# One attention-then-FFN kernel on one core: the outputs' scales in a column a chunk, k's features a slot behind q's, and some steps put first in the planner's order

## The chip, the cores and the metric

The kernel runs on one NeuronCore of a Trainium2 chip. A core has TensorE (PE, matrix products into PSUM; its weight loads are shown as PEld), VectorE (DVE), ScalarE (ACT), GpSimd (POOL) and SyncE (SP, which here issues most of the DMAs). Each engine has its own queue of instructions and takes them in order. The metric is device time of one execution in microseconds (us); lower is better.

## The reference, cut to what matters

```python
def phi(x):                                   # x: q or k, scaled by 64**-0.25
    proj = einsum('bhsd,md->bhsm', x, omega)  # 64 -> 128 features
    h = proj - sum(x * x, -1) / 2
    return exp(h - max(h, -1)) / sqrt(m)
kv  = einsum('bhsm,bhsd->bhmd', phi(k), v)
z   = sum(phi(k), over s)
num = einsum('bhsm,bhmd->bhsd', phi(q), kv)
den = einsum('bhsm,bhm->bhs',  phi(q), z) + 1e-6
x   = (num / den)  as (4608 tokens, 512)
out = ((x @ w1) * (x @ w2)) @ w3 @ w_out      # 512 -> 1024, gated, -> 512
```

8 batches, 8 heads, 576 positions, head width 64. All inputs are float32 or float64; every large product is made of float16 parts (high and low), three products for one.

## The kernel before, in words

The 4608 tokens are 36 chunks of 128. A batch is 576 tokens, that is four and a half chunks, so neighbouring batches share a chunk.

For each chunk of q and of k: a load (`load`, two buffers each of `qraw`, `kraw`), the sum of squares on ScalarE (`square_sum`, L158, tile `junk_q`/`junk_k`), its sum over partitions on TensorE and a power of two from it in four small VectorE steps (`power_of_two`, L163 to L178, and L232), the split into high and low parts (`split`, L141 on ScalarE and L144 on VectorE, tile `qhl`/`khl`), and then `features` (L250): projection on TensorE (`qpj`/`kpj`, L265), the maximum (`nm`, L275) and the subtraction (`qe`/`ke`, L288) on VectorE, the exponential on ScalarE (L289), and high and low parts again (L130, L132, L298), the low ones mostly on GpSimd.

k's features of a batch and v's parts (`vhl`) go into `kv_batch` (L339: matmuls `kvp`, L346, then high part on ScalarE, L355, and low part on VectorE, L356). q's features are transposed by DMA (`eqT`, L368) and go into `q_attend` (L370: matmuls `nu`, L381, then on VectorE gd, gr, xs, mx, L390 to L403). `x_turn` (L406) makes a power of two of mx, a scale `pt`, and the parts `xhl` (ScalarE L417, VectorE L418), which a DMA transposes into `xT` (L422).

The FFN of two chunks is four `gate` calls (48 matmuls each, L617, then asb on ScalarE and VectorE, L626 and L627, and parts on GpSimd, L631 and L632) and two `project_out` calls (24 matmuls `o`, L643). w3 and w_out are multiplied together once, in the opening (`wp`, L557), where all weights are also made from float64 words. `project_out` makes its output scale first (`osc`, L639), one number a token from `pt` and `kap`, in a small tile with four buffers; ScalarE reads it as it empties the bank (L647).

PSUM is in two pools: `ps_a`, two buffers of two banks, shared by qpj, kpj, kvp and nu; `ps_m`, four banks, shared by ab, o, the norms and the weights' products.

What sets the order. The program is written out slot by slot. Chunk step i begins at slot `begin[i]` = 3, 6, 9, ... for i = -5, -4, ... (the k chunk is i + 5, so k runs five chunks ahead of q). `put(slot, rank, fn)` files a piece of work; a slot issues its share of the weights, one unit of the FFN (`unit`), its pieces by rank, and one piece of v's work (`v_unit`). For step i: norms at begin - 3, scales at begin - 2, splits and next loads at begin - 1, q's features at begin (rank 1), k's at begin (rank 2), q_attend at begin + 5 (+ 2 for the first six), x_turn a slot after it, kv_batch five slots after its last k chunk (four or two for the first ones). v's eleven pieces of a batch (five sums, one scale, five splits) are queued when the second k chunk of the batch comes by; kv() runs what is left of them before it calls kv_batch.

That is the order of the program, and not yet that of an engine's queue. A planner plays the program through with a cost model before it is compiled; whenever an engine is free in that play, it takes the instruction that is ready there and has the lowest number, and the numbers go up in program order. The queues are then fixed. An instruction that was ready in the play and isn't on the chip makes its engine wait, with all that stands behind it. Inside `tc.high_priority()` an instruction gets the number of the program's start, so that it is taken first from the moment at which it is ready in the play.

Of the kernel before, what the change touches and what calls it, by code (L numbers as in the profile page):

```python
# [9 lines left out]
F32 = mybir.dt.float32  # L10
# [9 lines left out]
P = 128  # L20
# [30 lines left out]
EAGER = 40  # L51
EARLY = 6
KV_LAG = 5
RAW64_BUFS = 3
O_BUFS = 2
RAW_BUFS = 2
# [10 lines left out]
def tile_favor_attention_then_bilinear_ffn(  # L67
# [48 lines left out]
    def small(name, n=1, rows=P, dt=F32, bufs=4):  # L116
        return sm.tile([rows, n], dt, tag=f"s_{name}", name=name, bufs=bufs)
# [42 lines left out]
    def power_of_two(cols, n, name, pre=1.0, add=False, bufs=4):  # L160

        bank = bank_m(f"norm_{name}")
        nc.tensor.matmul(bank[:, 0:n], ones, cols, start=True, stop=True)  # L163
        t = bank[:, 0:n]
        if add:
            total = small("total")
            nc.vector.tensor_reduce(total, t, AX.X, ALU.add)
            t, n = total, 1

        q = bank[:, 16 : 16 + n]  # L170
        p = bank[:, 32 : 32 + n]

        nc.vector.tensor_scalar(
            q.bitcast(I32), t.bitcast(I32), 24, 23, ALU.logical_shift_right, ALU.logical_shift_left
        )
        nc.vector.tensor_scalar(p, q, 2.0**50 / pre, 2.0**-77 / pre, ALU.mult, ALU.max)
        s = small(f"s{n}_{bufs}", n, bufs=bufs)
        nc.vector.reciprocal(s, p)  # L178
        return p, s

    def pow2(val, n, name, bufs=4):

        p = small(f"p2p{n}_{bufs}", n, dt=I32, bufs=bufs)
        nc.vector.tensor_scalar(p, val.bitcast(I32), EXP_MASK, None, ALU.bitwise_and)
        p = p.bitcast(F32)
        r = small(f"p2r{n}_{bufs}", n, bufs=bufs)
        nc.vector.reciprocal(r, p)
        return p, r
# [150 lines left out]
    def kv_batch(b):  # L339
        t = at.tile([P, 2, H, E], F16, tag="kv", name=f"kv_{b}", bufs=3)  # L340
        cs = chunks_of(b)
        ps = banks(f"kvp_{b}")[:, :, 0 : 4 * E].rearrange("p g (i e) -> p g i e", e=E)
        for h in range(H):
            mm = [(c, x, y) for c, _, _ in cs for x, y in PASSES]
            for n, (c, x, y) in enumerate(mm):
                nc.tensor.matmul(  # L346
                    ps[:, h // 4, h % 4],
                    ek[c][:, x, place(h)],
                    vhl[b, c][:, y, h],
                    start=n == 0,  # L350
                    stop=n == len(mm) - 1,
                )
        ps = ps.rearrange("p g i e -> p g (i e)")
        hi, lo = (t[:, x].rearrange("p (g i) e -> p g (i e)", g=2) for x in range(2))
        nc.scalar.mul(hi, ps, 2.0**-19)  # L355
        nc.vector.scalar_tensor_tensor(lo, ps, 2.0**-19, hi, ALU.mult, ALU.subtract)  # L356
        kvs[b] = t

    xT, pts, eqs, xss = {}, {}, {}, {}
# [10 lines left out]
    def q_attend(c):  # L370

        t = eqs.pop(c)
        owners = [
            (b, max(b * S - c * P, 0), min((b + 1) * S - c * P, P))
            for b in range(c * P // S, ((c + 1) * P - 1) // S + 1)
        ]
        nu = banks(f"nu_{c}")[:, :, 0 : 4 * E].rearrange("p g (i e) -> p g i e", e=E)
        for h in range(H):
            for n, (x, y) in enumerate(PASSES):
                for b, r0, r1 in owners:  # L380
                    nc.tensor.matmul(  # L381
                        nu[r0:r1, h // 4, h % 4],
                        t[:, x, place(h), r0:r1],
                        kvs[b][:, y, h],
                        start=n == 0,
                        stop=n == 2,
                    )

        gd = small("gd", H)
        nc.vector.tensor_scalar_add(  # L390
            gd.rearrange("p (g i) -> p g i", g=2), nu[:, :, :, D], 1e-6 * M * 2.0**21
        )
        gr = small("gr", H)
        nc.vector.reciprocal(gr, gd)
        xs = at.tile([P, HD], F32, tag="xs", name=f"xs_{c}", bufs=1)
        nc.vector.tensor_tensor(  # L396
            xs.rearrange("p (g i d) -> p g i d", g=2, d=D),
            nu[:, :, :, 0:D],
            gr.rearrange("p (g i) -> p g i", g=2).unsqueeze(3).broadcast_to([P, 2, 4, D]),
            ALU.mult,  # L400
        )
        mx = small("mx")
        nc.vector.tensor_reduce(mx, xs, AX.X, ALU.max, apply_absolute_value=True)  # L403
        xss[c] = xs, mx, owners

    def x_turn(c):  # L406

        xs, mx, owners = xss.pop(c)
        nc.vector.tensor_scalar(mx, mx, TINY, 2.0**-12, ALU.max, ALU.mult)  # L409
        p, r = pow2(mx, 1, f"x{c}")  # L410

        pt = sm.tile([P, 1], F32, tag="pt", name=f"pt_{c}", bufs=14)
        for b, r0, r1 in owners:
            nc.vector.tensor_scalar(pt[r0:r1], p[r0:r1], pv[b][r0:r1], None, ALU.mult)
        pts[c] = pt
        t = at.tile([P, 2, HD], F16, tag="xhl", name=f"xhl_{c}", bufs=1)
        nc.scalar.mul(t[:, 0], xs, r)  # L417
        nc.vector.scalar_tensor_tensor(t[:, 1], xs, r, t[:, 0], ALU.mult, ALU.subtract)  # L418
        mc, off = c * P // TOK, c * P % TOK
        if mc not in xT:  # L420
            xT[mc] = at.tile([P, 2, NC, TOK], F16, tag="xT", name=f"xT_{mc}", bufs=XT_BUFS)
        nc.sync.dma_start_transpose(  # L422
            xT[mc].rearrange("p x c s -> p (x c) s")[:, :, off : off + P],
            t.rearrange("p x d -> p (x d)"),
        )

    w12b = const.tile([P, 2, 2 * NC + 1, 512], F32, name="w12b")
    Wb = const.tile([P, NF + 1, DO], F32, name="Wb")
# [175 lines left out]
    def gate(c0, n, u):  # L604
# [28 lines left out]
        for k in range(nf):  # L633
            for t in range(n):
                hs[c0 + t, u * nf + k] = h[:, :, k, t * P : (t + 1) * P], place

    def project_out(c):
        sc = small("osc")
        nc.vector.tensor_scalar(sc, pts[c], pts[c], kap, ALU.mult, ALU.mult)  # L639
        ps = bank_m(f"o_{c}")  # L640
        mm = [(f, a, b) for f in range(NF) for a, b in PASSES]
        for i, (f, a, b) in enumerate(mm):
            nc.tensor.matmul(ps, hs[c, f][0][:, a], W[f][:, b], start=i == 0, stop=i == len(mm) - 1)  # L643
        for f in range(NF):
            used(hs[c, f][1])
        o = mo.tile([P, DO], F32, tag="o", name=f"o_{c}", bufs=O_BUFS)
        nc.scalar.mul(o, ps, sc)  # L647
        nc.sync.dma_start(out[c * P : (c + 1) * P, :], o)
# [15 lines left out]
    def v_unit():  # L664
        if v_work:
            v_work.pop(0)[1]()
# [52 lines left out]
        plan.setdefault(slot, []).append((rank, len(plan[slot]) if slot in plan else 0, fn))  # L719

    behind_by = []

    def ready(c):
        x_turn(c)
# [14 lines left out]
    def step(i):  # L739
        at0 = begin[i]  # L740
        kc = i + LEAD
        keys = [(n, c) for n, c in (("q", i), ("k", kc)) if 0 <= c < NCH]
        state = {}

        def norms():
            state["am"] = norm(keys, i)

        def splits():
            for name, c in keys:
                split_raw(c, name)  # L750
                if c + 2 < NCH:
                    load(srcs[name], c + 2, name)

        put(at0 - 3, 3, norms)
        put(at0 - 2, 6, lambda: scale(keys, state["am"]))
        put(at0 - 1, 8, splits)
        if i >= 0:
            put(at0, 1, lambda: q_chunk(i))
            lag = 2 if i < EARLY else 5
            put(at0 + lag, 7 if i < EARLY else 0, lambda: q_attend(i))  # L760
            put(at0 + lag + 1, 0, lambda: ready(i))
        if kc < NCH:
            put(at0, 2, lambda: k_chunk(kc))
        if kc in B_OF_K:

            def kv():

                while v_work and v_work[0][0] <= B_OF_K[kc]:
                    v_unit()
                kv_batch(B_OF_K[kc])  # L770


            put(at0 + (2 if i < 0 else KV_LAG - 1 if i < EARLY else KV_LAG), 5, kv)
        for b in range(B):
            cs = [c for c, _, _ in chunks_of(b)]
            if cs[1] == kc:
                put(at0, 9, lambda b=b: v_batch(b))
            if cs[0] == kc:
                put(at0 + 2, 10, lambda cs=cs: [v_load(c) for c in cs if c not in vraw])
# [7 lines left out]
    for t in range(max(plan) + 1):  # L787
        n = min(PER[t] if t < len(PER) else 1, len(ticks))
        weights(n)
        if not ticks and raw_at:  # L790
            for a, w in [(a, 4) for a in raw_at] + [(a, 2) for a in mag_at]:
                free.extend(range(a, a + w))
            raw_at.clear()
        unit(RESERVE if t > EAGER else 0)
        for _, _, fn in sorted(plan.get(t, []), key=lambda x: x[:2]):
            fn()
        v_unit()
    assert not ticks
    while queue:
        unit()  # L800
# [38 lines left out]
```

## Time and profile before

| | |
|---|---|
| median of 3 runs | 906.85 us (904.66 to 910.05) |
| profiled execution | 904.25 us, of which the span is 902.5 us |
| mean granted TensorE clock | 0.951 |
| busy: PE / DVE / ACT / POOL | 790.9 / 622.6 / 421.0 / 322.2 us |
| DMA | 88.43 MB in 142525 packets |

All times in the profile are from the start of the span, in us. Instructions are named by engine, line of the kernel and operation, with output and input tiles by the names above; "idle before, <- X" is the time for which the engine stood still ahead of an instruction and what it waited for. Busy time of TensorE is modelled from the starts of pipelined matmuls. A clock of 1.00 is full speed.

### The profile page before, as it was taken

To read this page: it belongs to the slowest core of one execution; us is meant where nothing else is said; L and a number is where in the kernel's file an instruction comes from. 1 tells how busy PE (TensorE), PEld (TensorE's weight loads), DVE (VectorE), ACT (ScalarE), POOL (GpSimd) and SP (SyncE) were. 2 spreads that over 40 slices of the span, in tenths; PEclk is the share of its full clock that TensorE was granted. 3 is DMA by queue.
4 is the path that set the end of the run, shared out by engine and by line. 5 is a ranking of instruction groups with operands and counts; after the bars stand their busy time and mean duration, and the time that the engine had idled before them with its cause. 6 is when DMAs were issued, how large, how long until landed. Compare 5 with 4: busy or idle time off the path is not lost.

```text
span 902.5 us, 20601 instructions
## 1 busy us (share of the span) xinstructions
PE 790.9 (88%) x8614; PEld 586.0 (65%) x8614; DVE 622.6 (69%) x1116; ACT 421.0 (47%) x748; POOL 322.2 (36%) x327
## 2 busy tenths in 40 slices
PE   1964499578996998999999999899899899999998
PEld 0433254476875876767777776777677677677674
DVE  5879877788779887766867777778667774553210
ACT  3677874877436535444354335543454333221111
POOL 0000003223364465443634643455444543323221
PEclk9985699789999999999999999999999999999999
DMA  8535455332345353333434443344332232333000
GB/s 311 191 120 196 140 153 170 111 73 55 88 107 105 84 130 83 83 84 83 116 83 77 95 111 71 72 94 113 85 93 65 60 71 61 82 60 60 24 25 35
DMA packets 142525, 88.43 MB, mean 98 GB/s; under 512 B 116704, under 2 KB 116832, under 8 KB 142432
## 3 DMA queue, kind: packets, MB, share of 16 engines
q1 hardware_dynamic: 134944, 66.15, 31.0%
q10 hardware_dynamic: 7488, 20.97, 6.9%
q8 instruction: 67, 1.10, 0.5%
q14 instruction: 26, 0.21, 0.1%
HBM read 49.35 MB, written 9.44 MB: 65 GB/s over the span
## 4 chain that ended last, share of the span: by engine, by line
PE 42%; DVE 28%; ACT 13%; DMA 9%; issue 6%; POOL 1%; SPq 0%; DVEq 0%; ACTq 0%; POOLq 0%
PE ab L617 20%; PE o L643 11%; DVE nm L275 5%; DVE qhl L144 4%; DMA qraw<-qT 4%; PE wp L557 4%; DVE vhl L144 3%; ACT ke L289 2%; DVE qe L288 2%; DVE ke L288 2%; DMA kraw<-kT 2%; ACT ek L132 2%; PE kvp L346 2%; DVE asb L627 2%; PE nu L381 1%
## 5 line engine op out<-in xcount | busy, mean ns | idle before, releaser
L617 PE MATMUL ab<-xT,w12b 128*128 128x256 f16 (+1 forms) x3840 | 400.3, 265 | 10.8 <-DMA xT<-xhl 8.5
L617 PEld LDWEIGHTS <-w12b 128*128 128x128 f16 x3840 | 345.1, 99 | 54.3 <-issue 8.8
L643 PE MATMUL o<-Wb,arena 128*128 128x512 f16 x864 | 193.4, 379 | 2.1 <-DVE Wb L144 1.6
L643 PEld LDWEIGHTS <-arena 128*128 128x128 f16 x864 | 84.3, 100 | 96.3 <-issue 2.9
L631 POOL TENSOR_SCALAR arena<-asb 128x512 f16<-128x512 f32 x72 | 57.6, 800 | 249.7 <-DVE asb L627 238.3
L298 POOL TENSOR_TENSOR eq<-qe,eq 128x1024 f16<-128x1024 f32 x34 | 73.9, 2174 | 147.9 <-DVE eq L130 111.1
L289 ACT ACTIVATE qe<-qe,ln_e,es 128x1024 f32<-128x1024 f32 x31 | 38.4, 1239 | 138.0 <-DVE qe L288 138.0
L632 POOL TENSOR_TENSOR arena<-asb,arena 128x512 f16<-128x512 f32 x72 | 91.4, 1270 | 5.9
L627 DVE TENSOR_TENSOR asb<-ab,asb 128x512 f32<-128x512 f32 x72 | 49.4, 686 | 52.7 <-PE ab L617 50.6
L144 DVE SCALAR_TENSOR_TENSOR qhl<-qraw,s,qhl 128x512 f16<-128x512 f32 x36 | 63.8, 1773 | 28.7 <-ACT qhl L141 28.7
L158 ACT ACTIVATE junk_q<-qraw 128x512 bf16<-128x512 f32 x36 | 22.7, 630 | 120.4 <-DMA qraw<-qT 120.3
L298 POOL TENSOR_TENSOR ek<-ke,ek 128x1024 f16<-128x1024 f32 x28 | 60.2, 2149 | 41.4 <-DVE ek L130 39.8
L265 PE MATMUL kpj<-om,khl 64*128 64x128 f16 x864 | 36.9, 237 | 43.4 <-DVE xs L396 12.1
L639 DVE TENSOR_SCALAR osc<-pt,kap 128x1 f32<-128x1 f32 x36 | 9.5, 271 | 84.8 <-ACT o L647 84.6
L265 PEld LDWEIGHTS <-khl 64*128 64x128 f16 x864 | 29.4, 103 | 50.2 <-ACT junk_k L158 16.1
L557 PE MATMUL wp<-w12b 128*128 128x512 f32 x128 | 60.2, 623 | 1.2 <-DVE w12b L485 1.2
L626 ACT ACTIVATE asb<-ab 128x512 f32<-128x512 f32 x72 | 41.8, 580 | 24.4 <-PE ab L617 24.4
L381 PEld LDWEIGHTS <-eqT 128*128 128x128 f16 (+1 forms) x960 | 32.5, 102 | 26.0 <-DMA eqT<-eq 15.3
L647 ACT ACTIVATE o<-o,osc 128x512 f32<-128x512 f32 x36 | 24.2, 673 | 52.2 <-PE o L643 52.2
L381 PE MATMUL nu<-kv,eqT 128*128 128x65 f16 (+1 forms) x960 | 34.7, 196 | 15.0 <-DMA eqT<-eq 14.3
L418 DVE SCALAR_TENSOR_TENSOR xhl<-xs,p2r,xhl 128x512 f16<-128x512 f32 x36 | 28.8, 800 | 26.5 <-ACT xhl L417 26.4
L143 POOL TENSOR_SCALAR vhl<-vraw,s 128x512 f16<-128x512 f32 (+1 forms) x35 | 36.3, 1054 | 29.4 <-DVE mx L409 11.7
(124 smaller groups left out, 1071.1 us busy)
## 6 DMA issues: line engine op xcount, KB each, us to landing
kraw<-kT SPq DMA_DIRECT2D x36, 256.0 KB, 3.0
vraw<-v SPq DMA_DIRECT2D x36, 256.0 KB, 3.0
qraw<-qT SPq DMA_DIRECT2D x36, 256.0 KB, 2.7
out<-o SPq DMA_DIRECT2D x36, 256.0 KB, 2.0
arena<-w3T ACTq DMA_DIRECT2D x8, 1024.0 KB, 5.9
arena<-w ACTq DMA_DIRECT2D x8, 1024.0 KB, 5.6
arena<-wo ACTq DMA_DIRECT2D x4, 1024.0 KB, 5.1
eqT<-eq SPq DMA_TRANSPOSE x72, 3.1
```

The lines of the kernel that those rows point to most:

```text
L144: nc.vector.scalar_tensor_tensor(lo, src, s, hi, ALU.mult, ALU.subtract)
L265: nc.tensor.matmul(pg[:, g, i], hl[d, x, i], om[d, y], start=first is None and n == 0, stop=n == len(PASSES) - 1,)
L275: nc.vector.tensor_reduce(nm, pj, AX.X, ALU.max, negate=True)
L289: nc.scalar.activation(e, e, AF.Exp, scale=es, bias=ln_e)
L298: (nc.vector if lo == "d" else nc.gpsimd).tensor_tensor(t[:, 1], e, t[:, 0], ALU.subtract)
L381: nc.tensor.matmul(nu[r0:r1, h // 4, h % 4], t[:, x, place(h), r0:r1], kvs[b][:, y, h], start=n == 0, stop=n == 2,)
L557: nc.tensor.matmul(ps, w[:, j, k * P : (k + 1) * P], guest[:, j], start=j == j0, stop=j == HALF - 1,)
L617: nc.tensor.matmul(ps[:, k], w12[m][i][cc][:, a, r * P : (r + 1) * P], x[:, b, cc, off : off + T], start=j == 0, stop=j == len(mm) - 1,)
L627: nc.vector.tensor_tensor(asb, ab[1], asb, ALU.mult)
L631: nc.gpsimd.tensor_scalar(h[:, 0], asb, 1.0, 1.0, ALU.mult, ALU.mult)
L632: nc.gpsimd.tensor_tensor(h[:, 1], asb, h[:, 0], ALU.subtract)
L643: nc.tensor.matmul(ps, hs[c, f][0][:, a], W[f][:, b], start=i == 0, stop=i == len(mm) - 1)
```

## The change

```diff
+K_LATE = 8
...
 def power_of_two(...):
...
+        with tc.high_priority():
             q = bank[:, 16 : 16 + n]
             p = bank[:, 32 : 32 + n]
...
             nc.vector.tensor_scalar(p, q, 2.0**50 / pre, 2.0**-77 / pre, ALU.mult, ALU.max)
             s = small(f"s{n}_{bufs}", n, bufs=bufs)
             nc.vector.reciprocal(s, p)
...
 def kv_batch(b):
...
-        nc.scalar.mul(hi, ps, 2.0**-19)
-        nc.vector.scalar_tensor_tensor(lo, ps, 2.0**-19, hi, ALU.mult, ALU.subtract)
+        with tc.high_priority():
+            nc.scalar.mul(hi, ps, 2.0**-19)
+            nc.vector.scalar_tensor_tensor(lo, ps, 2.0**-19, hi, ALU.mult, ALU.subtract)
...
 def q_attend(c):
...
+        with tc.high_priority():
             gd = small("gd", H)
...
             nc.vector.tensor_reduce(mx, xs, AX.X, ALU.max, apply_absolute_value=True)
...
 def x_turn(c):
         xs, mx, owners = xss.pop(c)
+        with tc.high_priority():
             nc.vector.tensor_scalar(mx, mx, TINY, 2.0**-12, ALU.max, ALU.mult)
...
             nc.sync.dma_start_transpose(
                 xT[mc].rearrange("p x c s -> p (x c) s")[:, :, off : off + P],
                 t.rearrange("p x d -> p (x d)"),
             )
...
+    oscs = const.tile([P, NCH], F32, name="oscs")
+
     def project_out(c):
-        sc = small("osc")
+        sc = oscs[:, c : c + 1]
         nc.vector.tensor_scalar(sc, pts[c], pts[c], kap, ALU.mult, ALU.mult)
...
+    due = {}
...
-            put(at0, 2, lambda: k_chunk(kc))
+            put(at0 + (i >= K_LATE), 2, lambda: k_chunk(kc))
...
-            put(at0 + (2 if i < 0 else KV_LAG - 1 if i < EARLY else KV_LAG), 5, kv)
+            due[B_OF_K[kc]] = at0 + (2 if i < 0 else KV_LAG - 1 if i < EARLY else KV_LAG)
+            put(due[B_OF_K[kc]], 5, kv)
...
-        v_unit()
+
+        n = max([1] + [-(-(k + 1) // max(due[b] - t, 1)) for k, (b, _) in enumerate(v_work)])
+        for _ in range(n):
+            v_unit()
```

The steps that turn a norm into a power of two (behind its matmul and, for v and the weights, its sum), the two parts of kv, all VectorE steps behind `nu`, and the whole of `x_turn` with its DMA get the number of the program's start. The output scale of chunk c is column c of a constant tile of 36 columns in place of a small tile with four buffers. From step 8 on, k's features are issued one slot later, with the same rank. v's pieces are issued as many a slot as are needed to be done by the batch's due slot, one at least. No computation is added or taken away.

More of the change, by code (lines that the diff above doesn't have):

```diff
@@ L168, in power_of_two @@
             t, n = total, 1
[L170 to L178, printed above, removed]
+        with tc.high_priority():
+            q = bank[:, 16 : 16 + n]
+            p = bank[:, 32 : 32 + n]
+            nc.vector.tensor_scalar(
+                q.bitcast(I32), t.bitcast(I32), 24, 23, ALU.logical_shift_right, ALU.logical_shift_left
+            )
+            nc.vector.tensor_scalar(p, q, 2.0**50 / pre, 2.0**-77 / pre, ALU.mult, ALU.max)
+            s = small(f"s{n}_{bufs}", n, bufs=bufs)
+            nc.vector.reciprocal(s, p)
         return p, s
@@ L387, in q_attend @@
                     )
[L389 to L403, printed above, removed]
+        with tc.high_priority():
+            gd = small("gd", H)
+            nc.vector.tensor_scalar_add(
+                gd.rearrange("p (g i) -> p g i", g=2), nu[:, :, :, D], 1e-6 * M * 2.0**21
+            )
+            gr = small("gr", H)
+            nc.vector.reciprocal(gr, gd)
+            xs = at.tile([P, HD], F32, tag="xs", name=f"xs_{c}", bufs=1)
+            nc.vector.tensor_tensor(
+                xs.rearrange("p (g i d) -> p g i d", g=2, d=D),
+                nu[:, :, :, 0:D],
+                gr.rearrange("p (g i) -> p g i", g=2).unsqueeze(3).broadcast_to([P, 2, 4, D]),
+                ALU.mult,
+            )
+            mx = small("mx")
+            nc.vector.tensor_reduce(mx, xs, AX.X, ALU.max, apply_absolute_value=True)
         xss[c] = xs, mx, owners
@@ L408, in x_turn @@
         xs, mx, owners = xss.pop(c)
[L409 to L425, printed above, removed]
+        with tc.high_priority():
+            nc.vector.tensor_scalar(mx, mx, TINY, 2.0**-12, ALU.max, ALU.mult)
+            p, r = pow2(mx, 1, f"x{c}")
+            pt = sm.tile([P, 1], F32, tag="pt", name=f"pt_{c}", bufs=14)
+            for b, r0, r1 in owners:
+                nc.vector.tensor_scalar(pt[r0:r1], p[r0:r1], pv[b][r0:r1], None, ALU.mult)
+            pts[c] = pt
+            t = at.tile([P, 2, HD], F16, tag="xhl", name=f"xhl_{c}", bufs=1)
+            nc.scalar.mul(t[:, 0], xs, r)
+            nc.vector.scalar_tensor_tensor(t[:, 1], xs, r, t[:, 0], ALU.mult, ALU.subtract)
+            mc, off = c * P // TOK, c * P % TOK
+            if mc not in xT:
+                xT[mc] = at.tile([P, 2, NC, TOK], F16, tag="xT", name=f"xT_{mc}", bufs=XT_BUFS)
+            nc.sync.dma_start_transpose(
+                xT[mc].rearrange("p x c s -> p (x c) s")[:, :, off : off + P],
+                t.rearrange("p x d -> p (x d)"),
+            )
     w12b = const.tile([P, 2, 2 * NC + 1, 512], F32, name="w12b")
```

## The prediction

> **What bounds the kernel now.** I read the page first, then busy time by stretch, then who TensorE waits for, then one chunk in order of time.
>
> ```profile
> span 902.5 us, 20601 instructions
> ...
> PE 790.9 (88%) x8614; PEld 586.0 (65%) x8614; DVE 622.6 (69%) x1116; ACT 421.0 (47%) x748; POOL 322.2 (36%) x327
> ...
> PE 42%; DVE 28%; ACT 13%; DMA 9%; issue 6%; POOL 1%; SPq 0%; DVEq 0%; ACTq 0%; POOLq 0%
> ```
>
> TensorE is busy 88% of the span, yet it has only 42% of the chain that ended last. VectorE has 28% of it, so in some stretch VectorE's order holds TensorE. Which stretch (columns: length, then busy time and instructions of PE, PEld, DVE, ACT, POOL, granted clock, DMA share, GB/s):
>
> ```profile
> 320.00:760.00 440.00, 414.39 (x4780) 320.27 (x4779) 318.12 (x555) 190.91 (x313) 207.51 (x193) 0.98 0.37 87
> 0.00:320.00 320.00, 237.85 (x2631) 165.26 (x2631) 258.48 (x467) 203.94 (x396) 77.58 (x99) 0.89 0.48 135
> 760.00:902.00 142.00, 138.65 (x1210) 100.48 (x1207) 46.06 (x95) 26.14 (x39) 37.06 (x36) 1.00 0.21 47
> ```
>
> The last 142 us hold 3.4 us without TensorE work, and nothing there can be won. The middle holds 440 - 414.39 = 25.6 us of idle, the opening 320 - 237.85 = 82.2 us. In the middle, k's projection (tile kpj) has nearly all of it:
>
> ```profile
>   DVE xs L396: 10.9, 5
>   DVE kv L356: 9.2, 4
>   ACT junk_k L158: 5.3, 3
> ```
>
> 10.9 + 9.2 + 5.3 = 25.4 of the 25.6 us (the view of the tile in 320 to 760 us). A projection needs one of the two PSUM buffers of `ps_a`, and xs and kv are the last readers of a buffer that q_attend or kv_batch had. I take the third row for the same wait under another name. One chunk, in order of time (start, length, engine, line; in brackets the idle time before it):
>
> ```profile
> 541.40 0.28 PE L163 MATMUL norm_q_k<-sums,ones 128*128 128x3 f32 x2
> ...
> 544.70 0.16 DVE L173 TENSOR_SCALAR norm_q_k<-norm_q_k 128x3 int32<-128x3 int32 x1
> ...
> 546.60 2.44 DVE L144 SCALAR_TENSOR_TENSOR qhl<-qraw,s,qhl 128x512 f16<-128x512 f32 x1 [1.21 <-ACT qhl L141]
> 546.72 0.90 PE L381 MATMUL nu<-kv,eqT 128*128 128x65 f16 x24
> ...
> 549.97 0.15 DVE L390 TENSOR_SCALAR gd<-nu 128x8 f32<-128x8 f32 x1
> ...
> 550.16 0.20 DVE L394 RECIPROCAL gr<-gd 128x8 f32<-128x8 f32 x1
> ...
> 551.90 0.63 ACT L158 ACTIVATE junk_q<-qraw 128x512 bf16<-128x512 f32 x1 [4.72 <-DMA qraw<-qT]
> ...
> 552.53 0.67 ACT L647 ACTIVATE o<-o,osc 128x512 f32<-128x512 f32 x1
> ...
> 552.80 0.84 PE L265 MATMUL qpj<-om,qhl 64*128 64x128 f16 x24
> ...
> 553.23 0.27 DVE L639 TENSOR_SCALAR osc<-pt,kap 128x1 f32<-128x1 f32 x1 [2.86 <-ACT o L647]
> 553.42 0.68 DVE L396 TENSOR_TENSOR xs<-nu,gr 128x512 f32<-128x512 f32 x1
> ...
> 554.25 0.85 PE L265 MATMUL kpj<-om,khl 64*128 64x128 f16 x24 [0.60 <-DVE xs L396]
> ...
> 555.02 5.41 PE L617 MATMUL ab<-xT,w12b 128*128 128x256 f16 x48
> ...
> 555.31 0.19 DVE L414 TENSOR_SCALAR pt<-p2p,pv 128x1 f32<-128x1 f32 x1
> ...
> 557.26 0.75 DVE L418 SCALAR_TENSOR_TENSOR xhl<-xs,p2r,xhl 128x512 f16<-128x512 f32 x1 [1.76 <-ACT xhl L417]
> ...
> 560.42 5.34 PE L643 MATMUL o<-Wb,arena 128*128 128x512 f16 x24
> ...
> 562.31 1.23 DVE L288 TENSOR_TENSOR ke<-kpj,nm 128x1024 f32<-128x1024 f32 x1
> ...
> 566.33 3.79 PE L346 MATMUL kvp<-vhl,ek 128*128 128x65 f16 x120
> ...
> 578.55 0.70 DVE L356 SCALAR_TENSOR_TENSOR kv<-kvp,kv 128x520 f16<-128x520 f32 x1
> ...
> 579.40 0.85 PE L265 MATMUL kpj<-om,khl 64*128 64x128 f16 x24 [3.26 <-DVE kv L356]
> ```
>
> Read it as a ring. VectorE's osc takes a slot that ScalarE's o of four chunks before still reads; o stands behind junk_q; junk_q stands for 4.72 us until the qraw load lands; xs stands behind osc; kpj waits for xs. nu had been done at 546.72 + 0.90 = 547.62, and xs began 5.8 us later. The next kvp was done at 570.12, its kv at 579.25. Over the whole run:
>
> ```profile
> DVE osc L639 <- ACT o L647: 84.6, 28, 5.1
> ...
> ACT junk_q L158 <- DMA qraw<-qT: 120.3, 28, 5.5
> ...
> ACT xhl L417 <- DVE p2r L187: 28.4, 16, 2.7
> ...
> SPq L422 <- DVE asb L627: 63.8, 14, 5.6
> ...
> PE nu L381 <- DMA eqT<-eq: 14.3, 3, 8.9
> ...
> PE ab L617 <- DMA xT<-xhl: 8.5, 2, 6.3
> ```
>
> What can't shrink is TensorE's own work per chunk: two gate groups 2 x 5.41, o 5.34, q and k 0.84 + 0.85, nu 0.90, norms 0.28, and a kvp of 3.79 for 8 batches in 36 chunks = 0.84; together 19.9 us. 414.39 us of work at 19.9 us are 21 chunks, and 25.6 us of idle are 1.2 us in each. So the middle is bound by TensorE with small holes, and the holes (with what follows from them) are all that an order can win.
>
> **The change, part by part.**
>
> *A column a chunk for osc.* Nothing is computed more or less; the wait for o goes (84.6 us of VectorE idle). osc then needs only pt and kap. VectorE gets 2.86 us back in the chunk shown, and the stall doesn't pass to xs, whose operands (nu, gr) were there at 550.4: xs can run at once. Next late on VectorE is xhl, which waits for ScalarE behind junk_q (1.76 us here, more once it is reached earlier). kpj doesn't need xhl.
>
> *x's chain and kv's parts first.* gd to pt is 0.15 + 0.20 and 553.42 to 555.50 = 2.4 us; kv is 0.70. Placed as soon as nu and kvp end, they free the buffer some 5 to 8 us earlier. A wait is added in another form: VectorE may come to gd before TensorE has done nu, and behind it stand the splits of q and k. The transpose of xhl goes to the head of SP's queue as well, before the loads of qraw and kraw and the store of out. SP already stands 63.8 us at it (L422) behind VectorE, and the earlier xhl shortens that; I cost it at nothing. The cover: the next norms come a chunk after those at 541.40, about 561, and junk_q is done at 552.5; were it gone, a chunk would pay up to junk_q's 4.72 us. On ScalarE the first parts of xhl and kv go ahead too; xhl may stand there before its p2r (the 28.4 us row), and behind it asb and o, which free the four banks of `ps_m`. TensorE waits for no such bank in the middle, so again nothing.
>
> *The scales' steps first.* L173 began 544.70 - 541.68 = 3.0 us after its norms. Up to 3 us earlier scales mean earlier splits, loads and junk_q. On TensorE's path this is worth nothing by itself where qpj isn't waiting; the price if VectorE comes too early is a wait for the norms.
>
> *k's features one slot later.* From chunk 8 on (23 k chunks) a slot's unit of 5.3 to 5.4 us stands between qpj and kpj. The waits for a buffer before kpj were 3.26 us and below 4 us, so one unit covers each alone. VectorE's nm and ke of k move with it. No instruction is added.
>
> *v's parts spread.* Eleven parts a batch; batches start at slots 6, 18, 33, 45, 60, 72, 87, 99 and are due at 17, 31, 47, 59, 74, 86, 101, 113. At most 11 parts stand for at least 11 slots, so n is 1 in every slot, and the old loop in kv() finds none left. This part does nothing: 0 us.
>
> The terms, against the profiled execution (904.25 us, its span 902.5):
>
> - Holes before kpj: between 0 and -25.4. I take -20, near the upper end, because three edits act on the same wait and each would nearly do alone.
> - Clock. After a hole the gate runs slow:
>
> ```profile
> 349.25 1.46 PE L265 MATMUL kpj<-om,khl 64*128 64x128 f16 x24 [3.80 <-DVE xs L396]
> 350.65 6.26 PE L617 MATMUL ab<-xT,w12b 128*128 128x256 f16 x48
> ...
> 570.00:580.00 10.00, 6.74 (x98) 5.86 (x96) 5.55 (x15) 5.05 (x12) 1.48 (x12) 1.00 0.40 104
> ...
> 720.00:730.00 10.00, 9.84 (x84) 7.37 (x85) 8.90 (x18) 4.43 (x6) 2.72 (x3) 0.83 0.21 53
> ```
>
> 6.26 for 5.41 is 0.85 us. The middle's clock of 0.98 allows at most 0.02 x 440 = 8.8 us. Bounds 0 and -8.8; I take -4, about five holes of 0.85.
> - Opening: the two rows on eqT and xT are 14.3 + 8.5 = 22.8 us, of which x's earlier chain can touch the 8.5; the other way, VectorE is busy 258.48 of 320 us there and a step taken first delays another. Bounds -8.5 and +8.5; I take -2.
> - New waits on steps placed early: none in the trace. Bounds 0 and +33 (second rival); I take +3.
>
> Sum -23: 881.3 in that execution. The median of the runs, 906.85, is 2.6 above it, so 884 is predicted.
>
> The Trainium skill, "TensorE: Matmul & The Clock Gate", Part 1, says the array halves its clock after an idle window of about 3.4 us and needs a busy one to regain it. The 0.83 of a 10 us stretch is 3.4 us at half speed, as it says; that such a drop follows the 2.56 us hole at 720 and none the 3.26 us hole at 579 doesn't fit a plain threshold. By its 1.7 us a drop, estimated, the clock term would be about -8 in place of -4, and the sum 877.
>
> **The rivals.**
>
> *The wait moves to kvp (17%).* kpj now comes one slot before kvp, and kpj's buffer is held until ke ends: 562.31 + 1.23 - 554.25 = 9.3 us. From kpj to kvp there would be 0.85 + 5.4 + 0.90 = 7.1 us. Where VectorE is no quicker, each of the 6 batches of that time waits 2.2 us: +13, and the clock's 4 stay lost: 904.25 - 23 + 17 = 898, 901 on the scale of the median. For it: the hold in the trace. Against: VectorE sat 2.86 + 1.76 us of it on osc and xhl.
>
> *x's steps delay the splits: slower (11%).* If gd to pt, xhl's wait for ScalarE and xhl stand before qhl, the split is late by 2.4 + 1.76 + 0.75 = 4.9 us. It ended at 549.04 and qpj began at 552.80, so it decides from 3.8 us on. It would be 1.1 us late, or 2.2 with a stall of osc's 2.86 us in place of xhl's 1.76. With 1.6 us in each of 21 chunks it is +33 in place of the +3: 881.3 + 30 = 911, 914 on that scale. Against: qhl's operands are ready before nu is.
>
> *More than forecast (10%).* All holes (-25.4), the clock (-8.8) and half of the opening's 22.8 us: 904.25 - 45.6 = 859, so 861. Against: the opening waits on transfers and a full VectorE.
>
> **How the numbers follow.** The forecast has 62%, with its own range 870 to 897. Half a per cent, 4.5 us, is about what a measurement of this kernel can tell from no change: faster is below 902.3. The forecast, the third rival and a little under half of the first (whose 901 is at the bound) give 0.78; the rest of the first 0.11; the second 0.11. The range, 865 to 907, takes in the forecast, the first rival and the near side of the third, and leaves the second out.
>
> **What would show it.** Right: osc waits for nothing; kpj's idle in the middle is below 6 us; the middle's clock is 1.00; xs starts within 3 us of nu's end. Wrong: qpj waits for qhl or qhl for DVE gd (second rival); kvp or nu waits for DVE ke or nm (first); TensorE idle in the first 320 us moves by over 8 us either way; the number of v steps in a slot changes.

## The result, and the profile after

The changed kernel takes 872.49 us in the median of 4 runs (871.82 to 872.96), the kernel before 907.68 us in 4 (904.66 to 910.05): a ratio of 0.9613, with a 95% interval of 0.9583 to 0.9644. That is 35.2 us less, where 23 were forecast. The profiled executions took 904.25 and 872.62 us, 31.6 us apart; nearly all of the rest is that the one of before lay 3.4 us under its own median. One of the four executions of the run below with only the column took 4517.39 us, against 888 to 891 us in the other three, and is left out of its time.

The page of the changed kernel (its line numbers are up to 15 above those of before):

```profile
span 870.8 us, 20594 instructions
...
PE 787.7 (90%) x8608; PEld 582.9 (67%) x8614; DVE 614.1 (71%) x1116; ACT 416.9 (48%) x748; POOL 305.4 (35%) x327
...
PE 76%; DVE 10%; ACT 6%; DMA 4%; issue 3%; POOL 1%; ACTq 0%; SPq 0%; DVEq 0%; POOLq 0%
```

TensorE now has 76% of the chain that ended last in place of 42%. The span is 31.7 us shorter. By stretch, in the columns used before:

```profile
0.00:320.00 320.00, 240.74 (x2662) 169.28 (x2669) 259.91 (x469) 203.71 (x397) 77.87 (x101) 0.88 0.49 137
320.00:760.00 440.00, 440.00 (x5074) 336.53 (x5072) 325.23 (x589) 195.12 (x324) 202.05 (x200) 1.00 0.40 91
760.00:870.00 110.00, 107.00 (x877) 77.14 (x875) 28.98 (x60) 18.07 (x27) 25.45 (x26) 1.00 0.17 40
```

From 320 to 760 us TensorE has no idle left, and its clock is 1.00 there. That is 25.6 us. The clock gave more. Before, five holes of the middle were followed by products that took longer than their usual 0.84 us (a projection) and 5.41 us (a gate group). The prediction shows the first such place, at 349 us; these are the gate groups and projections of the other four:

```profile
392.80 0.97 PE L265 MATMUL kpj<-om,khl 64*128 64x128 f16 x24 [2.10 <-DVE kv L356]
393.71 6.91 PE L617 MATMUL ab<-xT,w12b 128*128 128x256 f16 x48
...
452.01 1.47 PE L265 MATMUL kpj<-om,khl 64*128 64x128 f16 x24 [2.68 <-DVE xs L396]
453.41 6.09 PE L617 MATMUL ab<-xT,w12b 128*128 128x256 f16 x48
...
496.04 1.47 PE L265 MATMUL kpj<-om,khl 64*128 64x128 f16 x24 [2.21 <-DVE kv L356]
497.44 6.25 PE L617 MATMUL ab<-xT,w12b 128*128 128x256 f16 x48
...
720.94 7.08 PE L617 MATMUL ab<-xT,w12b 128*128 128x256 f16 x48
```

The granted clock is 0.83 in each of the 10 us stretches from 390, 450, 490 and 720 us. Above the usual times, the five places lost 1.3 to 1.7 us each, 7.5 us together. No gate group or projection of the middle is slow in the changed kernel. What TensorE has left to do at 320 us is then 414.39 - 7.5 + 138.65 = 545.5 us before, and 440.00 + 107.00 = 547.0 us after, which is 1.5 us the other way. So the ledger is: holes of the middle -25.6, slow clock of the middle -7.5, the rest +1.5. The rest is less than what executions of the kernel before differ by (904.66 to 910.05), so these two traces can't tell whether the opening won or lost.

The busy time of the whole run (790.9 and 787.7 us) and the opening's idle (82.2 and 79.3 us) don't show this. A slow clock lengthens busy time, and the later trace lacks six matmuls of the opening: the group `l` has 16 before and 10 after, though all 16 of its weight loads are there. About 2 us of busy time are missing with them.

Of k's projection one wait is left between 250 and 760 us (the view of tile kpj on TensorE):

```profile
  DVE p2p L186: 0.5, 1
```

A place in order of time, the same engines and operations as in the prediction:

```profile
540.27 0.84 PE L267 MATMUL kpj<-om,khl 64*128 64x128 f16 x24
...
544.52 1.23 DVE L290 TENSOR_TENSOR ke<-kpj,nm 128x1024 f32<-128x1024 f32 x1
...
546.46 0.90 PE L384 MATMUL nu<-kv,eqT 128*128 128x65 f16 x24
...
547.20 3.79 PE L348 MATMUL kvp<-vhl,ek 128*128 128x65 f16 x120
...
547.67 0.75 DVE L145 SCALAR_TENSOR_TENSOR qhl<-qraw,s,qhl 128x512 f16<-128x512 f32 x1 [1.52 <-ACT qhl L142]
...
549.23 2.10 DVE L145 SCALAR_TENSOR_TENSOR khl<-kraw,s,khl 128x512 f16<-128x512 f32 x1 [0.81 <-ACT khl L142]
...
551.25 0.15 DVE L394 TENSOR_SCALAR gd<-nu 128x8 f32<-128x8 f32 x1
...
551.68 0.69 DVE L400 TENSOR_TENSOR xs<-nu,gr 128x512 f32<-128x512 f32 x1
...
553.81 0.27 DVE L647 TENSOR_SCALAR oscs<-pt,kap 128x1 f32<-128x1 f32 x1
...
556.16 0.84 PE L267 MATMUL qpj<-om,qhl 64*128 64x128 f16 x24
...
556.55 0.70 DVE L359 SCALAR_TENSOR_TENSOR kv<-kvp,kv 128x520 f16<-128x520 f32 x1
...
556.94 5.41 PE L622 MATMUL ab<-xT,w12b 128*128 128x256 f16 x48
...
562.28 0.84 PE L267 MATMUL kpj<-om,khl 64*128 64x128 f16 x24
```

No product of TensorE has a bracket here. osc runs without a wait, right behind pt. But xs begins 4.3 us after nu ends (547.36), not within 3: the split of k stands ahead of gd, though gd is to be taken first. kv is done 6.3 us after kvp (550.99 to 557.25; it was 9.1). That TensorE doesn't wait is owed to the place of kpj at 562.28: it now comes after qpj and a whole gate group, 5.0 us after kv is done.

What the two other engines wait for (whole run):

```profile
DVE gd L394 <- PE nu L384: 22.3, 8, 5.2
...
DVE xhl L423 <- ACT xhl L422: 11.4, 23, 1.7
...
ACT junk_q L159 <- DMA qraw<-qT: 56.5, 31, 5.3
ACT xhl L422 <- DVE p2r L189: 54.4, 28, 5.5
```

The 84.6 us at osc are gone. Part of them came back as a wait for TensorE itself (gd, 7.4 to 22.3 us), which costs nothing while TensorE is the bound. ScalarE stands 56.5 us for qraw in place of 120.3.

### The profile page after: what moved, and what is told of

Same layout as the page of the kernel before. It is cut to its first block, busy times and chain, and to the rows that moved or that the text cites. A ratio compares the mean times of both kernels' runs of the same rounds, so it can differ in the third digit from the quotient of the medians.

```text
span 870.8 us, 20594 instructions
## 1 busy us (share of the span) xinstructions
PE 787.7 (90%) x8608; PEld 582.9 (67%) x8614; DVE 614.1 (71%) x1116; ACT 416.9 (48%) x748; POOL 305.4 (35%) x327
## 4 chain that ended last, share of the span: by engine, by line
PE 76%; DVE 10%; ACT 6%; DMA 4%; issue 3%; POOL 1%; ACTq 0%; SPq 0%; DVEq 0%; POOLq 0%
PE ab L622 40%; PE o L651 20%; PE kvp L348 3%; PE nu L384 3%; PE wp L562 3%; PE qpj L267 3%; PE kpj L267 2%; DVE nm L277 1%; DVE vhl L145 1%; ACT qe L288 1%; DMA qraw<-qT 1%; ACT ke L288 1%; DVE arena L489 1%; DMA arena<-wo 1%; DVE w12b L490 1%
## 5 line engine op out<-in xcount | busy, mean ns | idle before, releaser
L636 POOL TENSOR_SCALAR arena<-asb 128x512 f16<-128x512 f32 x72 | 49.3, 685 | 217.9 <-DVE asb L632 207.3
L637 POOL TENSOR_TENSOR arena<-asb,arena 128x512 f16<-128x512 f32 x72 | 85.3, 1185 | 5.9
L291 ACT ACTIVATE ke<-ke,ln_e,es 128x1024 f32<-128x1024 f32 x27 | 33.5, 1241 | 79.0 <-DVE ke L290 62.4
L145 DVE SCALAR_TENSOR_TENSOR khl<-kraw,s,khl 128x512 f16<-128x512 f32 x36 | 53.9, 1497 | 16.2 <-ACT khl L142 16.2
L145 DVE SCALAR_TENSOR_TENSOR qhl<-qraw,s,qhl 128x512 f16<-128x512 f32 x36 | 32.1, 891 | 37.5 <-ACT qhl L142 37.5
L422 ACT ACTIVATE xhl<-xs,p2r 128x512 f16<-128x512 f32 x36 | 25.9, 719 | 58.1 <-DVE p2r L189 54.4
L159 ACT ACTIVATE junk_q<-qraw 128x512 bf16<-128x512 f32 x36 | 22.7, 630 | 56.5 <-DMA qraw<-qT 56.5
L655 ACT ACTIVATE o<-o,oscs 128x512 f32<-128x512 f32 x36 | 24.2, 673 | 50.6 <-PE o L651 50.6
L131 DVE CAST eq<-qe 128x1024 f16<-128x1024 f32 x31 | 22.1, 713 | 35.3 <-ACT qe L291 35.3
```

The lines of the kernel that those rows point to most:

```text
L145: nc.vector.scalar_tensor_tensor(lo, src, s, hi, ALU.mult, ALU.subtract)
L291: nc.scalar.activation(e, e, AF.Exp, scale=es, bias=ln_e)
L636: nc.gpsimd.tensor_scalar(h[:, 0], asb, 1.0, 1.0, ALU.mult, ALU.mult)
L637: nc.gpsimd.tensor_tensor(h[:, 1], asb, h[:, 0], ALU.subtract)
```

## The experiments

In all of them the kernel before was timed on the same chip; its medians were 905.59 us in the first four runs on record, 906.02 in the next four and 907.89 in the last four. The kernels that lack a part of the change lack v's part too, which changes nothing (below).

### The column for osc alone

```diff
-        sc = small("osc")
+        sc = oscs[:, c : c + 1]
```

> The kernel before with only the column a chunk for osc. Theory A (the prediction's: three edits act on the same wait ahead of kpj, and each nearly does alone): xs no longer stands behind osc, so the 10.9 us behind xs and the 5.3 us under junk_k go; the 9.2 us behind kv mostly stay, since ScalarE's part of kv still stands behind junk_v. About 888 us; VectorE waits at xhl for ScalarE over 40 us in all in place of 84.6 us at osc. Theory B (the ring through osc was the whole cause): within 4 us of the changed kernel, 872 to 877. Theory C (nothing but the later slot of k's features opens the buffer in time): within 5 us of 907.

Measured: 888.91 us in the median of three executions, 16.7 us less (the ratio on record is 0.9825, 0.9776 to 0.9873). Ahead of kpj, 250 to 760 us:

```profile
  DVE kv L356: 11.8, 4
  DVE khl L144: 1.5, 1
```

The waits behind xs and under junk_k are gone, the one behind kv isn't (9.2 to 11.8 us), and VectorE's wait at xhl rose from 26.4 to 53.8 us. This is theory A, to 1 us. The wait behind osc was real, but it was not the whole cause, as B had it, and C falls. It was also no ring through osc: with osc free, ScalarE still waits 118.4 us at junk_q for q's load (120.3 before). SyncE issues that load when VectorE's split of q has freed the tile (before, the split ends at 549.04 and the load is issued at 549.06), so the chain runs from the split to osc.

### k's later slot alone

```diff
-            put(at0, 2, lambda: k_chunk(kc))
+            put(at0 + (i >= K_LATE), 2, lambda: k_chunk(kc))
```

> The kernel before with only k's features one slot later from step 8 on. Theory A: a gate or output unit of 5.3 us stands between qpj and kpj and covers holes of at most 3.8 us; osc still waits some 60 us on VectorE. About 885 us, idle ahead of kpj between 320 and 730 us under 6 us. Theory B: VectorE still stands behind osc, the ring keeps its period and the holes move to other products: 900 to 907. Theory C: 872 to 877.

Measured: 877.46 us, ratio 0.9688 (0.9655 to 0.9721), 28.1 us less. By stretch, and what VectorE waits for:

```profile
0.00:320.00 320.00, 234.83 (x2617) 163.53 (x2624) 255.64 (x466) 202.12 (x394) 77.69 (x100) 0.89 0.48 136
320.00:760.00 440.00, 440.00 (x5074) 336.48 (x5073) 321.25 (x586) 197.86 (x327) 203.35 (x201) 1.00 0.40 92
```

```profile
DVE osc L640 <- ACT o L648: 29.0, 8, 5.1
```

The middle is closed at once and as completely as in the changed kernel. This edit alone is worth more than theory A gave it, and falls on the edge of C's figure; of what C claimed, only that the other edits are worth nothing alone was refuted by the run before. Nothing was done to osc, yet its wait went from 84.6 to 29.0 us. The trace shows how, in a place like the one of before:

```profile
553.05 0.67 ACT L648 ACTIVATE o<-o,osc 128x512 f32<-128x512 f32 x1
...
556.19 0.63 ACT L159 ACTIVATE junk_q<-qraw 128x512 bf16<-128x512 f32 x1 [2.47 <-DMA qraw<-qT]
```

ScalarE's o now stands ahead of junk_q, where before it stood behind it (551.90 and 552.53), so osc no longer waits for q's load here. ScalarE's wait for that load fell from 120.3 to 58.4 us in this run. What each of the two is worth was not tried by itself.

### The steps put first, alone

The four `with tc.high_priority():` blocks of the change, and nothing else of it.

> The kernel before with only the four groups of steps put first in the planner's order (scales, kv's parts, the steps behind nu, x_turn). Theory A: gd and xs come ahead of osc, so the buffer is freed early though osc waits as before: about 886 us. Theory B: the osc wait stands ahead of something else that TensorE needs: 898 to 907. The second rival of the prediction (the splits come late) would show here without k's later slot beside it: over 907, with qpj waiting for qhl.

Measured: 895.1 us, ratio 0.9877 (0.9842 to 0.9911), 10.5 us less: between the two theories. Ahead of kpj, and one chunk in order of time:

```profile
  DVE xs L399: 10.5, 7
  DVE kv L358: 7.8, 4
  ACT junk_k L158: 1.7, 2
```

```profile
542.33 0.20 DVE L397 RECIPROCAL gr<-gd 128x8 f32<-128x8 f32 x1
...
544.71 0.67 ACT L651 ACTIVATE o<-o,osc 128x512 f32<-128x512 f32 x1
...
545.41 0.28 DVE L643 TENSOR_SCALAR osc<-pt,kap 128x1 f32<-128x1 f32 x1 [2.88 <-ACT o L651]
545.60 0.68 DVE L399 TENSOR_TENSOR xs<-nu,gr 128x512 f32<-128x512 f32 x1
```

Theory A's reason is refuted: xs didn't come ahead of osc. The steps have the lowest numbers, and the planner still put osc between gr and xs; 20.0 of the 25.4 us stay. This fits the planner's rule given above, by which an instruction put first goes first only among what is ready at that moment of the play; the play itself was not looked at. Nor do the splits come late: TensorE's one wait for qhl after 250 us is the 4.9 us that the kernel before had too.

### The changed kernel without the column for osc

```diff
-        sc = oscs[:, c : c + 1]
+        sc = small("osc")
```

> The changed kernel with the small osc tile of four buffers back. Theory A: at most 5 us above the changed kernel (872 to 878), osc's wait back at over 40 us. Theory B: 895 to 907, for the ring is closed again. Theory C: as A.

Measured: 872.95 us, ratio 0.9637 (0.9607 to 0.9667); the changed kernel has 872.49. The column gives nothing measurable on top of the rest, though alone it gave 16.7 us. osc's wait comes back as 29.5 us, not as over 40, and no product of TensorE stands behind it.

### The changed kernel without the steps put first

The column and the later slot, without the four blocks.

> The changed kernel with no step put first: only the column for osc and k's later slot. Theory A2 (after the first four: k's later slot alone closes every hole of the middle, and the steps put first are worth what they do in the opening): 876 to 878, 4 to 5 us above the changed kernel, with no idle of TensorE between 320 and 760 us. Theory B2 (the steps put first are needed for nothing once k is late and osc is free): within 1.5 us of 872.5.

Measured: 877.72 us, ratio 0.969 (0.9668 to 0.9713). TensorE has 440.00 us of work between 320 and 760 us, so theory A2 holds: the blocks are worth some 5 us between the medians (2.7 us between the profiled executions), and all of it in the opening, for what TensorE has left at 320 us is 549.7 us here and 547.0 in the changed kernel.

### k's features two slots later

```diff
-            put(at0 + (i >= K_LATE), 2, lambda: k_chunk(kc))
+            put(at0 + 2 * (i >= K_LATE), 2, lambda: k_chunk(kc))
```

> The kernel before with k's features two slots later from step 8 on, in the slot of q_attend and kv_batch. Theory A2 (what counts is how many units of the FFN lie between the claims of a ps_a buffer): nu, kpj and kvp now claim two buffers within one slot, the holes come back, 10 to 25 us of idle in the middle, 890 to 905. Theory B2 (what counts is that VectorE's nm and ke of k no longer follow q's at once): they are apart here too, so 874 to 880.

Measured: 939.2 us, ratio 1.0365 (1.034 to 1.0391): 33 us slower than before. By stretch, what TensorE waits for from 250 us on, and a place in order of time:

```profile
320.00:760.00 440.00, 397.22 (x4404) 305.75 (x4403) 269.92 (x513) 178.92 (x297) 188.91 (x182) 0.94 0.35 82
```

```profile
PE kvp L347 <- DVE xs L397: 26.2, 5, 6.9
PE qpj L266 <- DVE xs L397: 17.8, 9, 3.9
```

```profile
585.88 0.90 PE L382 MATMUL nu<-kv,eqT 128*128 128x65 f16 x24
...
586.71 0.84 PE L266 MATMUL kpj<-om,khl 64*128 64x128 f16 x24
...
592.45 0.27 DVE L640 TENSOR_SCALAR osc<-pt,kap 128x1 f32<-128x1 f32 x1 [5.23 <-ACT o L648]
592.64 0.68 DVE L397 TENSOR_TENSOR xs<-nu,gr 128x512 f32<-128x512 f32 x1
...
593.38 5.76 PE L347 MATMUL kvp<-vhl,ek 128*128 128x65 f16 x120 [5.82 <-DVE xs L397]
```

nu and kpj take both buffers within a microsecond, and the third product, kvp or the next qpj, waits for xs behind osc. This is theory A2, with a larger price than it gave: 42.8 us of idle in the middle against 25.6 before, and a clock of 0.94. One slot closes every hole, two open wider ones. It is the distance in FFN units between the claims of a `ps_a` buffer that counts, not that k's work on VectorE is apart from q's. Nor is it that q's split got shorter (last section): its median is 0.87 us here and 2.38 us before, and the holes are wider.

### Two slots later, and the column for osc

The run before with `sc = oscs[:, c : c + 1]`.

> The kernel before with k's features two slots later from step 8 on and the column a chunk for osc. In the run without the column, nu, kpj and kvp claimed the two buffers within one slot, and kvp and qpj waited 26.2 and 17.8 us for xs, which stood behind osc. Theory A3 (the distance between claims sets how long a buffer may be held, and osc how long it is held): with osc free, xs runs at once and most of the 44 us go: 880 to 895. Theory B3 (the distance alone): the holes stay, 925 to 942.

Measured: 894.06 us, ratio 0.986 (0.9841 to 0.9879), 45 us less than without the column. What TensorE waits for after 320 us:

```profile
PE o L646 <- DVE asb L628: 8.3, 7, 2.9
PE kvp L347 <- DVE xs L397: 4.7, 4, 1.4
```

Theory A3 holds. The order of claims says how long a buffer may be held, osc how long it is held. Where the order leaves time, the wait at osc is harmless; where it leaves none, taking it away is worth 45 us.

### x's steps first, or the scales' steps first, beside k's later slot

Two kernels: the later slot with the blocks in q_attend and x_turn, and the later slot with the block in power_of_two.

> The kernel before with k's later slot and x's steps first (behind nu and x_turn), without the scales' and kv's. Theory A2 puts the last 4 to 5 us into the opening, and says nothing of which steps; if it is x's chain (the first gate waits 6.3 us for xT), 872 to 874; if it is the scales, 876 to 878.

> The kernel before with k's later slot and the scales' steps first, without x's and kv's. If the opening's gain comes from the scales (a split can start up to 3 us earlier, and the weights' split with it), 872 to 874; if it is x's chain, 876 to 878.

Measured: 874.33 us, ratio 0.9653 (0.9639 to 0.9667), and 872.63 us, ratio 0.9631 (0.9616 to 0.9645); without either 877.46 and 877.72. Each of the two has most of the 5 us or all of it, and both together have no more. Neither expectation had that: they do the same thing, or each lets the opening run into its next limit. Which, these runs don't tell.

### Three tries at the opening

Each is the changed kernel with one edit: `K_LATE = -5`, `K_LATE = 4`, and a string by which the low parts of k's first chunks alternate between VectorE and GpSimd (VectorE has six of them in place of eight, so two leave it and not the three to four of the expectation).

```diff
-EL = "ddddddpdpdpp"
+EL = "dpdpdpdpdpdpp"
```

> The changed kernel with k's features a slot later from the first step on (K_LATE -5). The opening still has 79 us of idle, among them 4.9 us of qpj for qhl near 275 us. If the order of q and k matters in the opening as in the middle: 866 to 871. If the opening is bound by VectorE and by transfers, and kv of the first batches comes a slot later: 872 to 880.

> The changed kernel with k's features a slot later from step 4 on in place of 8. Same question with the first four steps left as they are: 868 to 871 if the order matters between 160 and 270 us, 872 to 876 if not.

> The changed kernel with the low parts of k's first features alternately on VectorE and GpSimd (in the first six chunks all were on VectorE; GpSimd does almost nothing for the first 130 us). Three to four of 1.26 us leave VectorE, which is busy some 82% there. If VectorE's work bounds the opening: 867 to 871. If the two engines slow each other (qhl's split took 2.44 us beside GpSimd and 0.74 alone): 872 to 875.

Measured: 886.87 us (ratio 0.978, 0.9759 to 0.9801), 877.76 us (0.9677, 0.9659 to 0.9694) and 879.24 us (0.9692, 0.9674 to 0.9709), so all three are slower than the changed kernel. All have 440.00 us of work in the middle; what they lose, they lose before 320 us: behind 760 us TensorE has 122.5, 111.8 and 113.5 us left to do, against 107.0 in the changed kernel. In the first, a slot later for k from the start seems to delay all that follows; TensorE has 233.3 us of work in the opening against 240.7. Why the second loses is open: its busy time before 320 us is 241.0 us, no less than in the changed kernel. In the last the first gates wait longer for xT, which is 2.7 of the 6.6 us:

```profile
PE ab L622 <- DMA xT<-xhl: 9.2, 2, 8.6
```

against 6.5 us in the changed kernel. The changed kernel remains the fastest of those run. Level with it are the one without the column (872.95 us) and the one with only the later slot and the scales' block (872.63 us).

## Why the prediction was right, point by point

The direction, the place and the range were right; the size was short by over a quarter, 23 us forecast against 31.6 between the profiled executions. Term by term:

- **Holes before kpj**, -20 taken of at most -25.4: all 25.6 us of the middle's idle went. This term was mis-sized by 5.6 us, by caution alone; the sentence that one unit of 5.3 us covers each wait of below 4 us already said so, and the run with the later slot alone shows it.
- **Clock**, -4: the five slow places of the middle cost 7.5 us, and all of it went. The 0.85 us that the prediction took for each is what the gate group at 350.65 lost; the projection ahead of it lost another 0.62, and the gate groups at 393.71 and 720.94 lost 1.50 and 1.67. So the price of one was too low.
- **Opening**, -2: not decided. Between the profiled executions the rest is 1.5 us the other way; between the medians it is 35.2 - 25.6 - 7.5 = 2.1 us the way forecast, and executions of one kernel differ by more. The later slot alone has 440.00 + 110.63 = 550.6 us left at 320 us, some 5 us more than before, and its 28.1 us between the medians are 5 us less than the middle's 33.1; the steps put first win that back. This loss was not foreseen, and why it comes stays open.
- **New waits**, +3: none on TensorE in the middle. This term should have been 0 in the likeliest case.
- **2.6 us from the profiled execution to the median**: with a fourth run of the kernel before it is 3.4, and the changed kernel has none (872.62 profiled, 872.49 median). That adds 3.6 us to the difference of medians.

Holes, clock and new waits were all mis-sized to the same side, so the forecast doesn't hold by errors that cancel; it is short by their sum.

**"Three edits act on the same wait and each would nearly do alone"** was wrong as put. Alone they give 28.1 us (later slot), 16.7 (column) and 10.5 (steps first). The first closes the middle by itself, the second takes the part behind xs and leaves the part behind kv, and the third leaves 20.0 of 25.4 us. The step that failed is "placed as soon as nu and kvp end, they free the buffer some 5 to 8 us earlier": in the changed kernel gd stands behind the split of k, and xs comes 4.3 us after nu's end in place of 5.8. That the forecast held is owed to the slot, not to the planner's numbers. The "ring" is better read as a chain: q's split, q's load, junk_q, o, osc, xs, kpj (the run with the column alone).

**v's parts** do nothing, as worked out: n is 1 in every slot and kv() finds nothing left, so the program is written out the same without that part.

**The rivals.** The wait at kvp didn't come in the middle. Its 7.1 us from kpj to kvp are 6.9 (540.27 to 547.20), but the hold of 9.3 us is 5.5 (540.27 to 545.75). The reason given against it is right in part: the 1.76 us at xhl no longer lie in the hold. The 2.86 us at osc never did, for that wait ended at 553.23 and kpj began at 554.25. The rest is that kpj now begins when VectorE is done with x's chain and with q's maximum. With two slots in place of one kvp did wait, though for xs, which reads the buffer of nu, and not for ke. The splits weren't late: qhl ends at 548.42 and qpj begins at 556.16, 7.7 us of slack where 3.8 was the point of decision. The third rival's holes and part of its clock came, the opening's 11 us didn't.

**The clock rule.** It remains that a middle without holes runs at 1.00 and one with 42.8 us of them at 0.94. The five slow places came behind holes of 2.10 to 3.80 us, and none came behind those of 3.05 us (at 637 us) and 3.26 us, so no plain threshold on one hole fits. The rule of the Trainium skill ("TensorE: Matmul & The Clock Gate", Part 1) would, by the prediction's estimate of 1.7 us a drop, have put the clock's term at about -8. The trace agrees with that price better than with the -4 taken: 1.3 to 1.7 us a drop, 7.5 us in all.

## What to carry to other kernels

Where several products share a few PSUM buffers, write down for each claim what was claimed before it and how much of TensorE's own work lies between; here holes of up to 3.8 us closed by moving one claim behind one more unit, without making any engine faster, and moving it one unit further opened wider ones. Take a chain of waits apart into what makes a buffer be held and what makes it be wanted early: mending either one can hide the other, so the worth of an edit depends on which is already in. Price a slow clock by all products that it lengthens, not by the one that stands out. Putting an instruction first in a planner moves it only among what is ready there, so read the new order on the engine before counting on it.

## What the runs showed of the hardware

The split of q took 2.44 us in the prediction's chunk and 0.75 us in the changed kernel, the split of k 1.09 and 2.10 us. The groups say the same of all chunks:

```profile
L145 DVE SCALAR_TENSOR_TENSOR khl<-kraw,s,khl 128x512 f16<-128x512 f32 x36 | 53.9, 1497 | 16.2 <-ACT khl L142 16.2
...
L145 DVE SCALAR_TENSOR_TENSOR qhl<-qraw,s,qhl 128x512 f16<-128x512 f32 x36 | 32.1, 891 | 37.5 <-ACT qhl L142 37.5
```

The order moved 32 us of VectorE's time off q (63.8 before) and put 17 onto k (36.9 before). An instruction of the same form took from 0.70 to 2.62 us in the trace of before. GpSimd's low part of k, in order of time, before and then after:

```profile
546.35 2.13 POOL L298 TENSOR_TENSOR ek<-ke,ek 128x1024 f16<-128x1024 f32 x1
```

```profile
548.65 2.13 POOL L300 TENSOR_TENSOR ek<-ke,ek 128x1024 f16<-128x1024 f32 x1 [1.93 <-ACT ek L133]
```

Before, it lies over q's split (546.60 to 549.04), and after over k's (549.23 to 551.33). Over the traces of before, after and the run with two slots, the 104 of these splits that no TENSOR_TENSOR of GpSimd overlaps took 0.73 to 0.75 us each, and the 42 that took 2 us or more had 1.4 us or more of one beside them. Ten with 0.1 to 0.7 us of one beside them were no slower. No run took GpSimd's work away, so the cause is read off where the instructions lie, not shown by an experiment.
